# Expert stage: order of a tile's weights, the small slots' weights, the gates and the routing; gate weights moved behind attention

## The chip, the cores and the metric
The kernel runs on one core of a Trainium2 chip. Its time is the device time of one launch in microseconds; the kernel before has a median of 972.35 us over 3 runs (971.67 to 975.25). The engines are TensorE (PE, its weight loads as PEld), VectorE (DVE), ScalarE (ACT), GpSimd (POOL) and SyncE (SP), which issues most DMAs.

## The reference
All of it is float32. Three layers follow one another on 4 batches of 576 positions (2304 tokens, model width 512):
- attention, 8 heads of 64: `softmax(q k^T / 8, causal) v`, mixed with a memory term `phi(q) M / (phi(q) z + 1e-6)` by a gate per head, `g * mem + (1 - g) * local`, with g the sigmoid of `beta`;
- a dense layer: `h = x @ w_in` (512 to 2048), `h * clip(h + 3, 0, 6) / 6`, `@ w_out` (back to 512);
- an expert layer with 8 experts: `e = argmax(x @ w_gate)`, and for the tokens of expert e `gate_w * sigmoid(x @ w_output_gate[e]) * (relu(x @ w1[e]) @ w2[e])`, where `gate_w` is the softmax of the logits at e. Each w1 is 512x1024, each w2 1024x512.

## The kernel before, in words
**Accuracy.** A matmul operand is kept as two parts, high and low (names ending in H and L), and a product is three matmuls: high by high, high by low, low by high. For an expert's weights ACT casts the staged chunk to the high part (`high`, line 641) and DVE subtracts to get the low part (`low`, line 646).

**Attention and the first half of the dense layer** run together, from about 0 to 380 us. The order of their instructions on each engine is found by a planner from the program order, not written by hand. The gate weights `wg` (lines 409 to 411) are loaded near the start, cast on ACT and split on DVE into `wgs`; they are read for the first time by the logits in the second half of the dense layer, at 487 us.

**Routing.** After the last token block, `route()` counts the tokens of each expert, gives each token a slot, and makes index lists: `idx` (the rows that a tile of 128 tokens gathers), `idxs` (where its results go), `ei` and `sw` (a tile's expert, and whether it differs from that of the tile ahead of it). Nearly all of it is short DVE instructions. `route()` is a generator: each `next(routing)` runs it to the next `yield`, so the calls say between which matmuls its pieces stand. The two tiles of the expert that is found most loaded early (tiles 0 and 1) are computed beside it. `gates()` is the last token block's rest: a product with the gate's logits, an exponential on ACT (line 576), a reciprocal, and the store of the rows to `x2d`, from which the tiles gather.

**Tiles.** From `tiles(2, NR, ...)` on, tile i is computed while the weights of tile i + 1 are split. A tile is two groups of 12 matmuls for the hidden layer (`hidden`, line 688), two transposes of its result (line 667) and 24 matmuls for the output (`result`, line 701). `w.fetch` has SP issue 8 DMAs of 512 KB into staging buffers `st`; each has a condition, and where the next tile has the same expert it moves nothing. Its issue waits until the split has read the buffer for the last time. From here on the order on ACT, DVE, POOL and PE is the program's (`manual_schedule`); SP's is the planner's.

**Small slots.** An expert whose last tile holds at most 32 tokens gives these to one of four slots. Slot s is computed inside tile 4, 6, 9 or 11 (`HOSTS`). `small(s)` is a generator too: up to its first `yield` it reads the slot's expert (`esm`) on SP, gathers 32 rows (`sx`, POOL) and issues four loads of 512 KB (`sw<-w`, line 1020; the tile name `sw` is used twice). This is done one tile ahead. Each `tick()` in the host tile then runs one step: transposes, the hidden matmuls (line 1038) and the loads of the other four chunks (line 1022), a relu on ACT (`hq`, line 1043), transposes back, and the output matmuls (line 1056). A host tile has 17 ticks.

The lists of the slots (`idr`, `idq`, `esm`) are made in the last piece of `route()`, which runs at the end of tile 2.

Of the kernel before, what the change touches and what calls it, by code (L numbers as in the profile page):

```python
# [11 lines left out]
F32 = DT.float32  # L12
# [5 lines left out]
ALU = mybir.AluOpType  # L18
AX = mybir.AxisListType
# [3 lines left out]
P = 128  # L23
B, H, S, D = 4, 8, 576, 64
NT, DM, DFF = B * S, H * D, 2048
E, FF = 8, 1024
# [4 lines left out]
NS, SQ, SB = 4, 32, 4  # L31
NI = 24

NR = 19
HOSTS = {4: 0, 6: 1, 9: 2, 11: 3}
# [42 lines left out]
def f32(ap):  # L78
    return ap.bitcast(F32)
# [3 lines left out]
def tile_kernel(ctx, tc, qT, kT, qn, vx, z, beta, w_in, w_out, w_gates, w1, w2, out):  # L83
    nc = tc.nc
    PE, DVE, ACT, POOL, SP = nc.tensor, nc.vector, nc.scalar, nc.gpsimd, nc.sync
# [320 lines left out]
    DVE.memset(pz[:, :, D:], 1e-6)  # L406
    pairs[0].load()
    SP.dma_start(bt, beta.rearrange("(o h) -> o h", o=1).to_broadcast([P, H]))
    SP.dma_start(wg, w_gates.rearrange("(k p) e -> p k e", p=P))
    ACT.copy(wgs[:, :, : 2 * E], wg)  # L410
    DVE.tensor_tensor(wgs[:, :, 2 * E :], wg, f32(wgs[:, :, : 2 * E]), op=ALU.subtract)
    ACT.activation(gt, bt, AF.Exp, bias=0.0, scale=-1.0)
    DVE.tensor_scalar(gt, gt, 1.0, None, op0=ALU.add)
    DVE.reciprocal(gt, gt)
# [60 lines left out]
    for t in range(-1, len(pairs)):  # L475
        for x in PROGRAM.split():
            act(t, x)
    for _ in it:
        pass
    manual.close()  # L480
# [10 lines left out]
    k = 0  # L491
# [22 lines left out]
    part1, got = [], {}  # L514
# [98 lines left out]
    class Weights:  # L613
# [24 lines left out]
        def high(self, *cs):  # L638
            for c in cs:
                self.H[c] = self.pool.tile([P, 1024], F32R, name=f"wH{c}")  # L640
                ACT.copy(self.H[c], stage[c])  # L641
# [100 lines left out]
    def mid(x, n):  # L742

        return x.rearrange("p (o e) -> p o e", o=1).to_broadcast([P, n, x.shape[1]])

    def flat(x):
        return x.rearrange("p a b -> p (a b)")
# [72 lines left out]
    def route():  # L820
# [14 lines left out]
        DVE.tensor_reduce(cnt, tot, axis=AX.X, op=ALU.add)  # L835
        DVE.tensor_copy(tt, tot)
        DVE.tensor_tensor(gtc, cnt.to_broadcast([P, E, NJ]), mid(io18, E), op=ALU.is_gt)
        yield
        DVE.tensor_tensor_scan(flat(inc), onef, flat(tt), 0.0, op0=ALU.mult, op1=ALU.add)
        DVE.tensor_reduce(ntl, gtc, axis=AX.X, op=ALU.add)  # L840
# [33 lines left out]
        DVE.tensor_scalar(ci, pos, P - 1, None, op0=ALU.bitwise_and)  # L874
        DVE.tensor_scalar(ti, pos, 7, None, op0=ALU.arith_shift_right)
        DVE.tensor_copy(cf, ci)

        c1, c2 = (r2.tile([P, NI, E], F32, name=x) for x in ("c1", "c2"))
        DVE.tensor_tensor(c1, mid(flat(base), NI), itl.to_broadcast([P, NI, E]), op=ALU.is_le)
        DVE.tensor_copy(tf, ti)  # L880
        DVE.tensor_tensor(c2, mid(flat(end), NI), itl.to_broadcast([P, NI, E]), op=ALU.is_le)
        gates = got["gates"]
        next(gates)
        yield
        DVE.tensor_tensor(ohc[:, 0:6], mid(io128, 6), cf[:, 0:6].to_broadcast([P, 6, P]), op=ALU.is_equal)
        next(gates)
        DVE.tensor_tensor(c1, c1, c2, op=ALU.subtract)
        next(gates)
        DVE.tensor_tensor(ohc[:, 6:12], mid(io128, 6), cf[:, 6:12].to_broadcast([P, 6, P]), op=ALU.is_equal)
        next(gates)  # L890
        DVE.tensor_tensor(c1, c1, mid(io8, NI), op=ALU.mult)
        next(gates)
        yield
        DVE.tensor_tensor(ohc[:, 12:], mid(io128, NJ - 12), cf[:, 12:].to_broadcast([P, NJ - 12, P]), op=ALU.is_equal)
        yield
        ef = r2.tile([P, NI + 1, 1], F32, name="ef")
        DVE.memset(ef[:, 0:1], 0.0)
        DVE.tensor_reduce(ef[:, 1 : NI + 1], c1, axis=AX.X, op=ALU.add)
        rh = r2.tile([P, NJ, 3, NI + NS], BF16, name="rh")
        DVE.tensor_tensor(rh[:, :, 0], mid(ion, NJ), tf.to_broadcast([P, NJ, NI + NS]), op=ALU.is_equal)  # L900
        DVE.tensor_copy(ei, flat(ef)[:, 1 : NI + 1])
        DVE.tensor_tensor(sw, flat(ef)[:, 1 : NI + 1], flat(ef)[:, 0:NI], op=ALU.not_equal)
        DVE.tensor_scalar(rh[:, :, 1], rh[:, :, 0], iop, None, op0=ALU.mult)
        DVE.tensor_tensor(rh[:, :, 2], rh[:, :, 0], ioj.rearrange("p (j o) -> p j o", o=1).to_broadcast([P, NJ, NI + NS]), op=ALU.mult)
        yield
# [7 lines left out]
        DVE.scalar_tensor_tensor(tok, iv[:, 2], float(P), iv[:, 1], op0=ALU.mult, op1=ALU.add)  # L913
        DVE.tensor_copy(idx, tok)

        DVE.tensor_scalar(iv[:, 0], iv[:, 0], -1.0e6, 1.0e6, op0=ALU.mult, op1=ALU.add)
        DVE.tensor_tensor(tok, tok, iv[:, 0], op=ALU.add)
        DVE.tensor_copy(idxs, tok)
# [1 line left out]

        ivs = r.tile([P, 3, NS], BF16, name="ivs")
        DVE.tensor_copy(ivs, inv3[:, :, NI:])
        inq = ps_g.tile([P, 512], F32, name="inq", tag="pg")[:, : 3 * NS]
        PE.matmul(inq, lhsT=four, rhs=ivs.rearrange("p a n -> p (a n)"), start=True, stop=True)
        iq = r.tile([P, 3, NS], F32, name="iq")
# [5 lines left out]
        DVE.scalar_tensor_tensor(tks, tks, float(P // SQ), iq[:, 0], op0=ALU.mult, op1=ALU.add)  # L931
        DVE.tensor_scalar(tks, tks, qf, None, op0=ALU.add)
        DVE.tensor_copy(idq, tks)
        c3 = r.tile([P, NS, E], F32, name="c3")
        DVE.tensor_tensor(c3, mid(flat(key), NS), ion[:, 1 : NS + 1].rearrange("p (n o) -> p n o", o=1).to_broadcast([P, NS, E]), op=ALU.is_equal)
        DVE.tensor_tensor(c3, c3, mid(io8, NS), op=ALU.mult)
        ef3 = r.tile([P, NS, 1], F32, name="ef3")
        DVE.tensor_reduce(ef3, c3, axis=AX.X, op=ALU.add)
        DVE.tensor_copy(esm, flat(ef3))
        yield  # L940


# [46 lines left out]
    def hidden_out():  # L989
        return hp_.tile([P, FF], F32, name="hs"), [hp_.tile([P, 8, P], F32R, name=f"h{x}") for x in "HL"]  # L990
# [15 lines left out]
    def small(s):  # L1006


        er = SP.value_load(esm[0:1, s : s + 1], min_val=0, max_val=E - 1)
        xg = smp.tile([P, ROW], F32, name="sx")  # L1010
        POOL.indirect_dma_start(out=xg, out_offset=None, in_=x2d[:NT, :], in_offset=bass.IndirectOffsetOnAxis(ap=idr[:, s : s + 1], axis=0),
                                bounds_check=NT - 1, oob_is_err=False)
        ws = []

        def fetch():
            c = len(ws)
            if c < 2 * KD:
                w = smp.tile([P, 1024], F32, name="sw", bufs=SB)
                if c < KD:
                    SP.dma_start(w, w1[bass.ds(er, 1), c * P : (c + 1) * P, :].rearrange("o p f -> (o p) f"))  # L1020
                else:
                    SP.dma_start(w.rearrange("p (k d) -> p k d", k=2),
                                 w2[bass.ds(er, 1), 2 * (c - KD) * P : 2 * (c - KD + 1) * P, :].rearrange("o (k p) d -> (o p) k d", p=P))
                ws.append(w)

        for _ in range(SB):
            fetch()
        yield
        px = ps_g.tile([P, 512], F32, name="px", tag="pg")[:, : KD * SQ].rearrange("p (k t) -> p k t", k=KD)
        for k in range(KD):  # L1030
            PE.transpose(px[:, k], xg[:SQ, k * P : (k + 1) * P], ident[:SQ, :SQ])
        xT = smp.tile([P, KD, SQ], F32, name="xT")
        ACT.copy(xT, px)
        yield
        ph = ps_g.tile([P, 512], F32, name="ph", tag="pg")[:, : FF // 4]
        for k in range(KD):
            for g in range(4):
                PE.matmul(ph[g * SQ : (g + 1) * SQ, :], lhsT=xT[:, k], rhs=ws[k][:, g * 256 : (g + 1) * 256], start=k == 0, stop=k == KD - 1)
        while len(ws) < 2 * KD:
            fetch()  # L1040
        yield
        hq = smp.tile([P, FF // 4], F32, name="hq")
        ACT.activation(hq, ph, AF.Relu)
        yield
        pt = ps_g.tile([P, 512], F32, name="pt", tag="pg")[:, : 2 * P]
        for c in range(2):
            PE.transpose(pt[:, c * P : (c + 1) * P], hq[:, c * P : (c + 1) * P], ident)
        hT = smp.tile([P, 2, P], F32, name="hT")
        ACT.copy(hT, pt.rearrange("p (c t) -> p c t", c=2))
        for _ in range(9):  # L1050
            yield
        py = ps_g.tile([P, 512], F32, name="py", tag="pg")[:, :P]
        for g in range(4):
            for c in range(2):
                for q in range(4):
                    PE.matmul(py[q * SQ : (q + 1) * SQ, :], lhsT=hT[:, c, g * SQ : (g + 1) * SQ], rhs=ws[KD + g][:, c * 512 + q * P : c * 512 + (q + 1) * P],
                              start=g + c == 0, stop=g + c == 4)
        yield
        ys = smp.tile([P, P], F32, name="sy")
        ACT.activation(ys, py, AF.Copy, scale=xg[:, DM : DM + 1])  # L1060
        POOL.indirect_dma_start(out=out.rearrange("n (q d) -> (n q) d", q=4), out_offset=bass.IndirectOffsetOnAxis(ap=idq[:, s : s + 1], axis=0),
                                in_=ys, in_offset=None, bounds_check=4 * NT - 1, oob_is_err=False)
        yield
# [7 lines left out]
    def stepped(g, n):  # L1071

        for _ in range(n):
            r_ = next(g)
            tick()
        return r_

    def tiles(i0, i1, w, xg, xn, xx):
        nonlocal beside, smp
        for i in range(i0, i1):  # L1080
            if i + 1 in HOSTS and i + 1 < i1:
                ahead = small(HOSTS[i + 1])
                next(ahead)
            if i in HOSTS:
                beside = ahead
            more = i + 1 < i1
# [3 lines left out]
            xnn = rows(idx[:, i + 2 : i + 3]) if i + 2 < i1 else None  # L1090
            if more:
                w.fetch(0, 1, 2, 3, 4, 5, 7, 6)
            high, low = (w.high, w.low) if more else (lambda *cs: None,) * 2

            hs, hh = hidden_out()
            tick()
            ph = stepped(hidden(w0, xx, 0), 4)
# [8 lines left out]
            low(2)  # L1106
            DVE.tensor_tensor(hh[1][:, 0:4], px, f32(hh[0][:, 0:4]), op=ALU.subtract)
            ph = stepped(g, 2)
            high(3)
            relu(hs, ph, 1)  # L1110
            low(3)
# [108 lines left out]
```

## Time and profile before
| | |
|---|---|
| profiled execution | 975.48 us |
| its span, first to last instruction | 973.4 us |
| median of 3 runs | 972.35 us |
| PE busy | 915.6 us, 94% of the span |
| DVE, ACT, POOL busy | 627.7, 519.3, 370.5 us |
| mean granted TensorE clock | 0.978 |

The profile counts an instruction as busy from its start to its end; for PE, whose matmuls are pipelined, ends are modelled. "Idle before" is the time in which the engine had nothing running ahead of an instruction, and the name behind the arrow is what ended it. The granted clock of a stretch is a share of 2.4 GHz.

### The profile page before, as it was taken

How to read it: one execution, taken by the hardware profiler on the slowest of the kernel's cores; microseconds unless marked ns; L12 is line 12 of the kernel's file. 1: busy time of each engine (PE TensorE's matmuls, PEld its weight loads, DVE VectorE, ACT ScalarE, POOL GpSimd, SP SyncE). 2: the span in 40 equal slices, each digit the busy share in tenths (PEclk: the TensorE clock that was granted, in tenths of full speed). 3: DMA queues.
4: the chain of work that ended last, by engine and by line, in shares of the span. 5: the costliest groups of instructions: out<-in, count | busy, mean ns of one | idle time of the engine just before them, and what ended most of it. 6: DMA issues, size and time to landing. Idle time of an engine off the chain costs nothing. (4 is left out here: it accounts for less than half of the span.)

```text
span 973.4 us, 17053 instructions
## 1 busy us (share of the span) xinstructions
PE 915.6 (94%) x5733; PEld 721.7 (74%) x5733; DVE 627.7 (64%) x1511; ACT 519.3 (53%) x1084; POOL 370.5 (38%) x574
## 2 busy tenths in 40 slices
PE   5788889999999999899999999998997999999996
PEld 3445667777777778779988888887775777778785
DVE  6889996576556533686344444448766769668982
ACT  5677665565555454444222222223345768668883
POOL 2636556465555443245433333336021212112210
PEclk9989899999999999899999999999999999999998
DMA  5434432121212003443011111113223664633850
GB/s 181 139 112 146 131 100 74 52 86 52 78 54 90 14 23 109 130 131 108 1 45 44 44 44 45 44 44 138 80 77 120 218 250 176 208 131 119 311 205 23
DMA packets 49277, 101.69 MB, mean 104 GB/s; under 512 B 5341, under 2 KB 15581, under 8 KB 49184
## 3 DMA queue, kind: packets, MB, share of 16 engines
q1 hardware_dynamic: 45696, 89.74, 27.3%
q0 software_dynamic: 3488, 10.80, 3.3%
q8 instruction: 47, 0.77, 0.3%
q14 instruction: 46, 0.38, 0.1%
HBM read 136.66 MB, written 14.72 MB: 156 GB/s over the span
## 5 line engine op out<-in xcount | busy, mean ns | idle before, releaser
L646 DVE TENSOR_TENSOR wL<-st,wH 128x1024 fp32r<-128x1024 f32 x136 | 163.7, 1227 | 42.7 <-ACT wH L641 41.5
L95 POOL TENSOR_SCALAR gH<-g 128x256 fp32r<-128x256 f32 x144 | 65.5, 455 | 271.4 <-DVE g L217 213.5
L213 PE MATMUL hps<-xH,wH 128*128 128x256 f32 x576 | 167.3, 291 | 1.5 <-ACT xH L91 1.0
L213 PE MATMUL hps<-xL,wH 128*128 128x256 f32 x576 | 163.0, 283 | 2.4 <-DVE xL L200 2.4
L213 PE MATMUL hps<-xH,wL 128*128 128x256 f32 x576 | 161.7, 281 | 0.0
L365 POOL TENSOR_SCALAR a<-a,rs,omg 128x320 f32<-128x320 f32 (+4 forms) x160 | 128.1, 812 | 78.0 <-DVE rs L360 52.1
L217 DVE SCALAR_TENSOR_TENSOR g<-g,hps 128x256 f32<-128x256 f32 x144 | 60.0, 417 | 146.4 <-ACT g L216 146.4
L641 ACT CAST wH<-st 128x1024 fp32r<-128x1024 f32 x136 | 139.7, 1053 | 8.4 <-DMA st<-w 8.3
L216 ACT ACTIVATE g<-hps,half 128x256 f32<-128x256 f32 x144 | 68.1, 473 | 139.2 <-PE hps L213 116.0
L213 PEld LDWEIGHTS hps<-xH,wH 128*128 128x128 f32 x576 | 109.5, 191 | 18.3 <-issue 12.6
L221 POOL TENSOR_TENSOR gL<-g,gH 128x256 fp32r<-128x256 f32 x144 | 115.8, 804 | 11.7
L213 PEld LDWEIGHTS hps<-xL,wH 128*128 128x128 f32 x576 | 109.8, 191 | 8.4 <-DVE xL L200 3.4
L352 ACT ACTIVATE a<-st,mn 64x64 f32<-64x64 f32 (+4 forms) x160 | 88.4, 555 | 43.9 <-DVE mn L343 43.8
L213 PEld LDWEIGHTS hps<-xH,wL 128*128 128x128 f32 x576 | 109.8, 191 | 0.1
L182 PE MATMUL acc<-wH,gH 128*128 128x512 f32 x288 | 95.8, 414 | 0.2 <-POOL gH L95 0.2
L337 PE MATMUL pa<-kd,qd 64*128 64x64 f32 (+5 forms) x384 | 82.1, 470 | 13.8 <-DVE mn L343 8.7
L182 PE MATMUL acc<-wH,gL 128*128 128x512 f32 x288 | 91.6, 400 | 2.3 <-POOL gL L221 2.3
L182 PE MATMUL acc<-wL,gH 128*128 128x512 f32 x288 | 91.0, 398 | 0.0
L376 PE MATMUL pa<-ident,a 128*128 128x128 f32 (+1 forms) x480 | 75.3, 289 | 13.3 <-DVE mn L343 8.0
L376 PEld LDWEIGHTS pa<-ident,a 128*128 128x128 f32 (+1 forms) x480 | 55.6, 145 | 37.1 <-DVE mn L343 14.0
L708 POOL DMA_INDIRECT out<-ys,idxs x17 | 19.2, 1128 | 124.7 <-ACT ys L707 69.4
L182 PEld LDWEIGHTS acc<-wH,gL 128*128 128x128 f32 x288 | 54.3, 190 | 15.9 <-POOL gL L221 3.1
(239 smaller groups left out, 1720.8 us busy)
## 6 DMA issues: line engine op xcount, KB each, us to landing
st<-w SPq DMA_DIRECT2D x136, 512.0 KB
sw<-w SPq DMA_DIRECT2D x32, 512.0 KB
w<-w_in SPq DMA_DIRECT2D x16, 512.0 KB
w<-w_out SPq DMA_DIRECT2D x16, 512.0 KB
qnt<-qn SPq DMA_DIRECT2D x16, 320.0 KB
vt<-vx SPq DMA_DIRECT2D x16, 320.0 KB
x2d<-row SPq DMA_DIRECT2D x18, 258.0 KB
qd<-qT SPq DMA_DIRECT2D x16, 288.0 KB
```

The costliest lines, as they stand in the source:

```text
L95: POOL.tensor_scalar(out, x, 1.0, 1.0, op0=ALU.mult, op1=ALU.mult)
L182: PE.matmul(acc[t], lhsT=gg[:, t * P : (t + 1) * P], rhs=ww[:, 512:1024], start=m == 0 and first, stop=m == HM - 1 and last)
L213: PE.matmul(hps, lhsT=ww[:, kk * P : (kk + 1) * P], rhs=xx[:, kk], start=k == 0, stop=k == 3 * KD - 1)
L216: ACT.activation(g, hps, AF.Relu, bias=half, scale=1.0 / 6.0)
L217: DVE.scalar_tensor_tensor(g, g, 1.0, hps, op0=ALU.min, op1=ALU.mult)
L221: ENG[GL].tensor_tensor(gL, g, f32(gH), op=ALU.subtract)
L337: PE.matmul(pss[j][: QN[i], o : o + k1 - k0], lhsT=self.qd[r, QS[i] : QS[i] + QN[i]], rhs=self.kd[r, k0:k1], start=True, stop=True)
L352: ACT.activation(self.a[j][:m, o + D : o + D + n], self.st[j][i][:m, :n], AF.Exp, bias=self.mn[j][:m, i : i + 1], scale=-1.0, accum_out=se ...
L365: ENG[NORM[i]].tensor_scalar(av, av, r[:m, i], omg[:m, h : h + 1], op0=ALU.mult, op1=ALU.mult)
L376: PE.transpose(psa[:, off : off + QN[i]], self.a[j][: QN[i], QO[i] + c * P : QO[i] + (c + 1) * P], ident[: QN[i], : QN[i]])
L641: ACT.copy(self.H[c], stage[c])
L646: DVE.tensor_tensor(self.L[c], stage[c], f32(self.H[c]), op=ALU.subtract)
```

## The change
- `wg` is loaded, cast and split behind the program of attention instead of near the start.
- In `route()`, `gates()` begins in the second piece instead of the third, and the instructions that make `ei` and `sw` (lines 879 to 902) stand behind those that make `idx`.
- The slots' lists get two pieces instead of one: `esm` first, `idr` and `idq` second. They are run in tile 2 ahead of its first and of its second half's `high(3)`.
- One tile ahead of a host, `w.fetch` comes first, then the put and the gather of the tile, and `small(...)` behind them.
- In the host, the slot's relu and transposes come four ticks later, and its output matmuls one tick later.

```diff
     SP.dma_start(bt, beta.rearrange("(o h) -> o h", o=1).to_broadcast([P, H]))
-    SP.dma_start(wg, w_gates.rearrange("(k p) e -> p k e", p=P))
-    ACT.copy(wgs[:, :, : 2 * E], wg)
-    DVE.tensor_tensor(wgs[:, :, 2 * E :], wg, f32(wgs[:, :, : 2 * E]), op=ALU.subtract)
...
             act(t, x)
+    SP.dma_start(wg, w_gates.rearrange("(k p) e -> p k e", p=P))
+    ACT.copy(wgs[:, :, : 2 * E], wg)
+    DVE.tensor_tensor(wgs[:, :, 2 * E :], wg, f32(wgs[:, :, : 2 * E]), op=ALU.subtract)
...
         DVE.tensor_tensor(gtc, cnt.to_broadcast([P, E, NJ]), mid(io18, E), op=ALU.is_gt)
+        gates = got["gates"]
+        next(gates)
         yield
...
-        c1, c2 = (r2.tile([P, NI, E], F32, name=x) for x in ("c1", "c2"))
-        DVE.tensor_tensor(c1, mid(flat(base), NI), itl.to_broadcast([P, NI, E]), op=ALU.is_le)
         DVE.tensor_copy(tf, ti)
-        DVE.tensor_tensor(c2, mid(flat(end), NI), itl.to_broadcast([P, NI, E]), op=ALU.is_le)
-        gates = got["gates"]
-        next(gates)
         yield
...
         DVE.tensor_copy(idx, tok)
+        c1, c2 = (r2.tile([P, NI, E], F32, name=x) for x in ("c1", "c2"))
+        DVE.tensor_tensor(c1, mid(flat(base), NI), itl.to_broadcast([P, NI, E]), op=ALU.is_le)
+        DVE.tensor_tensor(c2, mid(flat(end), NI), itl.to_broadcast([P, NI, E]), op=ALU.is_le)
+        DVE.tensor_tensor(c1, c1, c2, op=ALU.subtract)
+        DVE.tensor_tensor(c1, c1, mid(io8, NI), op=ALU.mult)
+        ef = r2.tile([P, NI + 1, 1], F32, name="ef")
+        DVE.memset(ef[:, 0:1], 0.0)
+        DVE.tensor_reduce(ef[:, 1 : NI + 1], c1, axis=AX.X, op=ALU.add)
+        DVE.tensor_copy(ei, flat(ef)[:, 1 : NI + 1])
+        DVE.tensor_tensor(sw, flat(ef)[:, 1 : NI + 1], flat(ef)[:, 0:NI], op=ALU.not_equal)
...
         DVE.tensor_copy(ivs, inv3[:, :, NI:])
+        c3 = r.tile([P, NS, E], F32, name="c3")
...
+        DVE.tensor_copy(esm, flat(ef3))
+        yield
         inq = ps_g.tile([P, 512], F32, name="inq", tag="pg")[:, : 3 * NS]
...
         while len(ws) < 2 * KD:
             fetch()
         yield
+        for _ in range(4):
+            yield
         hq = smp.tile([P, FF // 4], F32, name="hq")
...
-        for _ in range(9):
+        for _ in range(6):
             yield
...
         for i in range(i0, i1):
-            if i + 1 in HOSTS and i + 1 < i1:
-                ahead = small(HOSTS[i + 1])
-                next(ahead)
             if i in HOSTS:
                 beside = ahead
...
             if more:
                 w.fetch(0, 1, 2, 3, 4, 5, 7, 6)
+            if i + 1 in HOSTS and i + 1 < i1:
+                ahead = small(HOSTS[i + 1])
+                next(ahead)
             high, low = (w.high, w.low) if more else (lambda *cs: None,) * 2
+            if i == 2:
+                next(routing)
             hs, hh = hidden_out()
...
             ph = stepped(g, 2)
+            if i == 2:
+                next(routing)
             high(3)
```

## Rows read from the trace of the kernel before
**Rows 1.** Busy time by stretch: PE, PEld, DVE, ACT, POOL, clock, DMA share, GB/s.
```profile
884.92:898.29 13.37, 13.37 (x67) 10.82 (x66) 11.93 (x13) 11.59 (x15) 2.52 (x2) 1.00 0.32 117
```
**Rows 2.** PE's waits from 655 us on: total us, times, longest.
```profile
PE px L667 <- ACT hs L693: 7.7, 6, 3.8
...
PE py L701 <- DVE hL L1107: 1.1, 4, 0.3
```
**Rows 3.** Timeline in tile 3: start, length, engine, line, operation [idle before, releaser].
```profile
736.64 2.08 SPq L1020 DMA_DIRECT2D sw<-w  x4
...
739.14 13.97 SPq L636 DMA_DIRECT2D st<-w  x16
739.23 1.99 ACT L641 CAST wH<-st 128x1024 fp32r<-128x1024 f32 x2 [6.32 <-DMA st<-w]
...
741.77 0.66 PE L667 MATMUL px<-ident,hs 128*128 128x128 f32 x4 [3.84 <-ACT hs L693]
```
**Rows 4.** Timeline of the routing, beside tile 1.
```profile
703.79 0.35 DVE L879 TENSOR_TENSOR c<-base,itl 128x192 f32<-128x192 f32 x1
...
704.81 0.20 ACT L576 ACTIVATE so<-so 128x2 f32<-128x2 f32 x1 [8.00 <-DVE so L575]
...
706.13 0.66 PE L667 MATMUL px<-ident,hs 128*128 128x128 f32 x4 [0.85 <-ACT hs L693]
...
710.81 0.85 PE L908 MATMUL inv<-rh,ohc 128*128 128x84 bf16 x18 [1.40 <-DVE rh L904]
```
**Rows 5.** Timeline in tile 4, the first host.
```profile
756.81 0.37 ACT L1049 COPY hT<-pt 128x256 f32<-128x256 f32 x1 [1.40 <-PE pt L1047]
...
759.63 0.66 PE L667 MATMUL px<-ident,hs 128*128 128x128 f32 x4 [0.76 <-ACT hs L693]
```
**Rows 6.** Timeline at the end of tile 2, where the slots' lists are made.
```profile
733.25 0.17 DVE L922 CAST ivs<-inv 128x12 bf16<-128x12 f32 x1
733.47 0.17 PE L924 MATMUL inq<-ivs,four 128*128 128x12 bf16 x1 [1.29 <-DVE ivs L922]
...
735.56 0.17 DVE L939 CAST esm<-ef 128x4 int32<-128x4 f32 x1
```
**Rows 7.** Busy time by single microseconds behind that stall, the clock among it.
```profile
742.00:743.00 1.00, 1.00 (x7) 0.91 (x6) 0.97 (x2) 1.00 (x2) 0.00 (x0) 0.88 0.93 360
743.00:744.00 1.00, 1.00 (x4) 0.71 (x4) 1.00 (x2) 1.00 (x2) 0.00 (x0) 0.50 1.03 422
...
746.00:747.00 1.00, 1.00 (x8) 0.76 (x7) 0.80 (x1) 0.17 (x1) 0.00 (x0) 0.92 0.29 99
```
**Rows 8.** Timeline of POOL around the second host's gather.
```profile
769.10 1.02 POOL L1061 DMA_INDIRECT out<-sy,idq  x1 [13.86 <-ACT sy L1060]
...
775.30 2.00 POOL L708 DMA_INDIRECT out<-ys,idxs  x1 [3.37 <-ACT wH L641]
```
**Rows 9.** Timeline at the start of the kernel.
```profile
2.67 0.43 SPq L408 DMA_DIRECT2D bt<-beta  x1
3.15 0.43 SPq L409 DMA_DIRECT2D wg<-w_gates  x1
...
9.23 0.24 ACT L410 CAST wgs<-wg 128x64 fp32r<-128x64 f32 x1 [2.68 <-DMA wg<-w_gates]
...
9.65 0.17 DVE L413 TENSOR_SCALAR gt<-gt 128x8 f32<-128x8 f32 x1
```
**Rows 10.** Busy time behind the start, columns as in rows 1.
```profile
20.00:140.00 120.00, 99.37 (x571) 64.15 (x570) 109.22 (x325) 79.53 (x209) 64.77 (x96) 0.91 0.40 127
```
**Rows 11.** The slots' gathers: from issue to landing.
```profile
DMA to landing us min/median/max: 4.7/6.2/7.4
```
**Rows 12.** Busy time by stretch, from the loads ahead of three hosts on.
```profile
764.00:782.00 18.00, 18.00 (x143) 14.48 (x142) 14.48 (x15) 14.35 (x19) 5.99 (x4) 1.00 0.45 164
...
803.00:826.00 23.00, 23.00 (x112) 18.50 (x111) 20.82 (x21) 20.34 (x26) 6.23 (x5) 1.00 0.50 187
842.00:858.00 16.00, 16.00 (x109) 12.96 (x98) 12.80 (x14) 13.24 (x18) 4.57 (x4) 1.00 0.54 184
```

More of the change, by code (lines that the diff above doesn't have):

```diff
@@ L886, in route @@
         next(gates)
-        DVE.tensor_tensor(c1, c1, c2, op=ALU.subtract)
         next(gates)
@@ L890, in route @@
         next(gates)
-        DVE.tensor_tensor(c1, c1, mid(io8, NI), op=ALU.mult)
         next(gates)
@@ L895, in route @@
         yield
-        ef = r2.tile([P, NI + 1, 1], F32, name="ef")
-        DVE.memset(ef[:, 0:1], 0.0)
-        DVE.tensor_reduce(ef[:, 1 : NI + 1], c1, axis=AX.X, op=ALU.add)
         rh = r2.tile([P, NJ, 3, NI + NS], BF16, name="rh")
         DVE.tensor_tensor(rh[:, :, 0], mid(ion, NJ), tf.to_broadcast([P, NJ, NI + NS]), op=ALU.is_equal)
-        DVE.tensor_copy(ei, flat(ef)[:, 1 : NI + 1])
-        DVE.tensor_tensor(sw, flat(ef)[:, 1 : NI + 1], flat(ef)[:, 0:NI], op=ALU.not_equal)
         DVE.tensor_scalar(rh[:, :, 1], rh[:, :, 0], iop, None, op0=ALU.mult)
@@ L922, in route @@
         DVE.tensor_copy(ivs, inv3[:, :, NI:])
+        c3 = r.tile([P, NS, E], F32, name="c3")
+        DVE.tensor_tensor(c3, mid(flat(key), NS), ion[:, 1 : NS + 1].rearrange("p (n o) -> p n o", o=1).to_broadcast([P, NS, E]), op=ALU.is_equal)
+        DVE.tensor_tensor(c3, c3, mid(io8, NS), op=ALU.mult)
+        ef3 = r.tile([P, NS, 1], F32, name="ef3")
+        DVE.tensor_reduce(ef3, c3, axis=AX.X, op=ALU.add)
+        DVE.tensor_copy(esm, flat(ef3))
+        yield
         inq = ps_g.tile([P, 512], F32, name="inq", tag="pg")[:, : 3 * NS]
@@ L933, in route @@
         DVE.tensor_copy(idq, tks)
[L934 to L939, printed above, removed]
         yield
```

## The prediction
> **What bounds the kernel now.** I read the busy shares first: PE works for 94% of the span, so a change pays only where PE stands still or its clock is low. Next came busy time by stretch. A stretch of plain tiles has PE busy without a gap at full clock, DVE for 11.93 of 13.37 us and ACT for 11.59 [rows 1]: nothing that shortens DVE, ACT or DMA there moves the end. Then PE's waits from the routing on: it waits six times, 7.7 us in all, for `hs` from ACT, longest 3.8, and four times, 1.1 us, for the low part of `hs` from DVE [rows 2]. The timeline says where. One wait is tile 3's, 3.84 [rows 3]; one is the routing's, 0.85 [rows 4]; the other four, 0.76 each, are the hosts' [rows 5] (3.84 + 0.85 + 4 x 0.76 = 7.73). The reader is to see that each is a question of order on a queue: in none of them is the engine that PE waits for short of time.
>
> **The change part by part.** The sum is made against the profiled execution, 975.48 us (span 973.4); the median is 3.13 lower.
>
> *Tile 3.* SP issues the first slot's loads at 736.64, then tile 4's weights at 739.14. ACT had stood idle for 6.32 us and begins at 739.23, 0.09 after that first issue: these DMAs move nothing (same expert), so ACT waited for their issue and for no bytes. Its cast stands ahead of `relu` on ACT, and so PE waits 3.84 until 741.77 [rows 3]. SP stood behind `esm`, which DVE wrote at 735.56 [rows 6], because `small` came first in the program. With the fetch first, these eight issues wait only for their staging buffers, which the split frees during tile 2. The 3.84 goes. So does what follows it: the granted clock is 0.88 in the microsecond from 742, 0.50 in the three from 743 (the first stands) and 0.92 in that from 746 [rows 7], 2.4 GHz falling to 1.2 after the idle stretch. What is missing to 1 there is lost: 0.12 + 3 x 0.50 + 0.08 = 1.7. Sum 5.5. Nothing else is late there: tile 3's rows were gathered in the routing, and the slot's inputs are wanted only a tile later.
>
> *End of tile 2.* `inq` on PE waits 1.29 us for `ivs`, queued on DVE behind the last low parts [rows 6]. Both lists now come earlier in tile 2, and that wait goes. The price: seven short DVE instructions of 0.17 (as the cast of `esm` [rows 6]), 1.2 us, now stand in front of `low(3)` in a tile where DVE has little idle time. The low part of the second half of `hs` comes about 1.2 later, and its matmul is the seventh behind the transposes: I estimate some 0.7 to spare and take 0.5 lost, bounds 0 and 1.2. Net 0.8 (0.1 to 1.3).
>
> *Routing.* `so` on ACT waits 8.00 us for DVE, with `ys` and `hs` behind it, and PE waits 0.85 [rows 4]. With `gates` begun one piece earlier that wait goes. It is not an extra gain: PE then reaches the matmuls of `inv` sooner and waits there, as it does now, 1.40 for `rh` [rows 4]. What moves `inv` is DVE's chain. Eight instructions leave it; five of them go over 192 columns, 0.35 each [rows 4], at most 1.75 end to end; ends overlap the next one's start, and the three small ones are left out. The three DVE instructions of `gates` stay in the chain, so moving them is worth nothing by itself. I take 1.3. Behind `idx` the moved instructions delay the low part of `hs` that `result` wants; PE loses there what a full clock could have won, so 0.9 to 1.9. `ei` and `sw` come some 3 us later on SP, and tile 3's fetch with them; it moves nothing, and its first cast stands behind `ys`, so it is covered.
>
> *Hosts.* ACT waits 1.40 for the slot's transposes [rows 5], with `high(0, 1)` and `relu` queued behind; PE then waits 0.76 for `hs` and 0.3 for the low part [rows 2, 5]. Four ticks later, `hq` stands behind `relu` and `high(2)`, where its matmuls are long done. Four hosts: 4 x 1.04 = 4.2. ACT has two more short copies (0.37 each, as `hT` [rows 5]) in front of `high(3)` and the second `relu`, which I price at 0.15 a host: 3.6 (2.5 to 4.2). The output matmuls one tick later still have three ticks.
>
> *Slots' inputs.* The loads now stand behind the tile's eight issues, the last of which waits for the last low part, so they go out some 5 to 7 us later than at 736.64 and its like; 2.1 MB at 422 GB/s [rows 7] take 5 us, and they are wanted a whole tile after. On POOL the gather stands behind the put and the tile's gather. At the second host the put waits for the slot's stores: from 769.10 to 775.30 [rows 8]. I cost both at nothing, cover about 1 us for the gather and 3 for the loads; without it PE, strictly in order here, stands still.
>
> *Start.* ACT waits 2.68 for `wg`, then casts it for 0.24 ahead of `gt`, and DVE's `gt` begins at 9.65 [rows 9]. Of the 120 us from 20 on DVE is busy for 109.22, PE for 99.37 [rows 10]: DVE is the nearest to full there, and I let the start's gain pass on whole. Next in line is `bt`. If that lands only as `wg` does, 0.2 is won; if it is there when ACT would first ask, at 6.55 (9.23 less 2.68), it is 2.85 (9.65 less 6.8). `bt` was issued 0.48 ahead of `wg` [rows 9], and I give it that lead: 0.7. The split behind attention is 0.5 us of work on two engines that have slack there, long ahead of its reader. The planner's order may shift elsewhere; I have no row for that and let the range bear 1.5 either way.
>
> Sum: 5.5 + 0.8 + 1.3 + 3.6 + 0.7 = 11.9. The profiled execution becomes 963.6, the median 972.35 - 11.9 = 960.5.
>
> **The rivals.**
> 1. *The fetch still comes late.* SP's order is the planner's; it could still issue `sw` ahead of `st`. For it: SP is not among the engines ordered by hand. Against it: before, SP followed the program, `sw` then `st` [rows 3]. Without 5.5 the median is 966.0.
> 2. *The slots' gather is late.* Last on POOL, behind a put that waited 6.2 us for the slot's stores [rows 8], it would be issued some 8 us into the tile and land 7.4 later at worst [rows 11], 15.4. It is wanted when the tile ends: 60 matmuls at 13.37 / 67 each [rows 1] are 12.0, with the joints some 12.4. PE stands 3 at hosts two and four, with 1.7 each of half clock as in tile 3: 9.4, so 970; at the median landing of 6.2 it is 3.6, so 964. Against it: that put waited while the slot's loads filled the DMA engines, and these now come later. The Trainium skill (DMA: Bandwidth & Descriptors, section Queues, rings and completion order) says that each DMA engine takes turns between the queues by packet; by that a gather would not wait for all of the loads in front of it, and this rival would cost little. The landings of 4.7 to 7.4 agree in that none is as long as the loads.
> 3. *More at the start*: `bt` there at once, 2.85, and 1.9 in the routing: 2.8 more, 957.7.
> 4. *The order of loads turns against the hosts: slower.* Where the tile after really changes expert, 4.2 MB now go ahead of the slot's 2.1 MB: 10 us at 422 GB/s in front of loads with 3 us to spare. PE would stand some 7 us a host. Two hosts eat the gain, from there on it is slower; four cost 28 and give 988. For it: the loads are now behind. Against it: ahead of the second to fourth host 18 us at 164 GB/s are 3.0 MB, 23 at 187 are 4.3 and 16 at 184 are 2.9 [rows 12]; the loads and the rows of the tiles fill these, the middle one with the end of an earlier tile's fetch, so no fetch of 4.2 MB stands there, nor at the first host [rows 3].
> 5. *No change*: rivals 1 and 2 together, 11.9 - 5.5 - 5 to 6 = about 1, so 971.
>
> **How the numbers follow.** Forecast 0.61, rival 1 0.09, rival 2 0.11, rival 3 0.10, rival 4 0.04, rival 5 0.05. A measurement of this kernel tells 0.5% (4.9 us) from no change. Faster: the forecast and rivals 1 to 3, less 0.01 for the worst of rival 2, 0.90. Same: 0.06. Slower: 0.04. The forecast's own range is 956.5 to 963.5. At the low end stands 956 (between the forecast and all its bounds at once, 957.7 less the hosts' 0.6 and the planner's share); the high end takes in rival 1 and the milder rival 2, 967.5.
>
> **What would show it.** In the changed trace: tile 4's `st` issued by SP ahead of the first `sw`, no wait of ACT for `st`, PE's waits for `hs` down from 7.7 to under 1, full clock through tiles 2 to 4; `inq` inside tile 2; the `inv` matmuls about 2 us earlier against the kernel's start (1.3 of the routing's and 0.7 of the start's); each host about 0.9 shorter. A wait of PE for `sx` or the slot's `sw` would show rivals 2 or 4; the first block of dense matmuls coming later than before would say that the planner's new order costs more than the start gives.

## The result, and the profile after

The changed kernel takes 962.05 us (median of 4 runs, 960.27 to 963.5), the kernel before beside it 972.01: ratio 0.9889, 95% interval 0.9862 to 0.9917. Timed again it took 962.99 us (6 runs, 959.75 to 965.45) against 974.09, ratio 0.9887 [0.986, 0.9913]. So 10 to 11 us were won. The profiled execution is 961.85 us, its span 959.9.

PE's waits from 640 us on, of the kernel after (engine and line, what it waited for: total us, times, longest):

```profile
PE acc L182 <- POOL gL L221: 2.3, 1, 2.3
PE py L701 <- DVE hL L672: 1.5, 2, 0.8
PE inv L897 <- DVE rh L893: 1.1, 1, 1.1
PE pi L815 <- DVE ohc L812: 0.6, 1, 0.6
PE py L701 <- ACT hH L671: 0.4, 1, 0.4
PE pf L760 <- DVE ohb L822: 0.4, 1, 0.4
```

Against [rows 2], both of those waits are gone: no `px` for `hs`, 7.7 before, and no `py` for the low part of the hosts' `hs`. Two new ones stand in the list, both in the routing: 1.5 for a low part (L672) and 0.4 for a high part (L671).

SP's queue in tiles 2 to 4, and, with the columns of [rows 1], the stretch in which the granted clock (third from the end) had been 0.50 to 0.92 [rows 7]:

```profile
714.66 17.66 SPq L636 DMA_DIRECT2D st<-w  x16
733.18 2.14 SPq L1021 DMA_DIRECT2D sw<-w  x4
736.91 7.81 SPq L636 DMA_DIRECT2D st<-w  x8
```
```profile
742.00:746.00 4.00, 4.00 (x42) 2.49 (x44) 3.30 (x4) 3.68 (x6) 1.23 (x2) 1.00 0.02 7
```

The sixteen `st` of tiles 3 and 4 are issued before the first `sw`; before, tile 4's stood behind it [rows 3]. The profile's group of ACT's casts shows what that ended: idle before them 2.0 us in all, 1.9 of it for `st`; before, it was 8.4 and 8.3. Tile 3's 6.3 of it is gone. What is left stands ahead of 712 us, and so do the 3.6 of a second profile of the changed kernel.

```profile
L641 ACT CAST wH<-st 128x1024 fp32r<-128x1024 f32 x136 | 139.6, 1052 | 2.0 <-DMA st<-w 1.9
```

The slots' lists in tile 2, and the first host (answers to [rows 6] and [rows 5]):

```profile
719.07 0.31 DVE L928 CAST esm<-ef 128x4 int32<-128x4 f32 x1
...
723.73 0.18 PE L931 MATMUL inq<-ivs,four 128*128 128x12 bf16 x1
```
```profile
748.96 0.60 ACT L693 ACTIVATE hs<-ph 128x512 f32<-128x512 f32 x1 [2.71 <-PE ph L688]
...
750.10 0.60 PE L667 MATMUL px<-ident,hs 128*128 128x128 f32 x4
750.39 0.39 ACT L1046 ACTIVATE hq<-ph 128x256 f32<-128x256 f32 x1
...
751.66 0.37 ACT L1052 COPY hT<-pt 128x256 f32<-128x256 f32 x1 [0.33 <-PE pt L1050]
...
752.88 0.61 ACT L693 ACTIVATE hs<-ph 128x512 f32<-128x512 f32 x1
...
753.55 0.64 PE L667 MATMUL px<-ident,hs 128*128 128x128 f32 x4
```

`inq` has no bracket: PE stands idle for nothing in front of it. ACT waits 0.33 for the slot's transposes, not 1.40. The transposes at 750.10 are those that waited 0.76 for `hs` before [rows 5]; the first `hs` now stands ahead of the slot's relu on ACT, and PE doesn't wait. Nor does it at 753.55, the transposes of the second half, whose `hs` now has the slot's copies in front of it.

Where the time went, stage by stage. Marks: DVE's first row sum of the dense layer's second half (483.06 us in the profile before), its last one (685.36), and the end of a tile, which is the start of ACT's `ys`; the last row ends with that of the last tile. Gains in us, against the profile of before; the second column is a second profile of the changed kernel.

| stage | predicted | profile after | second profile |
|---|---|---|---|
| to the first row sum (start) | 0.7 | -0.35 | -0.12 |
| to the last row sum | 0 | 1.42 | -0.10 |
| to the end of tile 1 (routing) | 1.3 | 0.63 | 0.08 |
| tile 2 | -0.5 | -0.38 | -0.39 |
| tile 3 | 5.5 + 1.3 | 7.06 | 7.03 |
| to the end of the last tile (four hosts) | 3.6 | 5.28 | 5.27 |
| sum | 11.9 | 13.66 | 11.77 |

The two profiles differ where the clock does. Busy time and clock of the two places, before, after, and after once more:

```profile
681.00:685.00 4.00, 3.50 (x11) 2.86 (x12) 0.69 (x1) 1.39 (x2) 1.56 (x3) 0.57 1.05 402
712.00:716.00 4.00, 4.00 (x14) 3.19 (x13) 1.46 (x6) 0.59 (x1) 2.05 (x2) 0.57 0.35 82
```
```profile
681.00:685.00 4.00, 3.15 (x16) 2.57 (x16) 1.54 (x4) 1.94 (x3) 1.91 (x3) 1.00 1.04 400
712.00:716.00 4.00, 3.17 (x14) 2.26 (x13) 2.10 (x10) 0.25 (x1) 1.55 (x2) 1.00 0.47 132
```
```profile
681.00:685.00 4.00, 3.17 (x10) 2.64 (x11) 0.64 (x2) 1.06 (x2) 1.88 (x3) 0.57 1.04 402
712.00:716.00 4.00, 4.00 (x14) 3.21 (x13) 3.35 (x15) 0.58 (x1) 2.15 (x2) 0.57 0.27 70
```

The first profile after had full clock in both stretches; the second had, like the kernel before, half clock for most of each (0.57 over 4 us is 4 x 0.43 / 0.5 = 3.4 us at 0.50). So like stands against like in the last column, and the 1.42 and 0.63 of the first are not the change's.

### The profile page after: what moved, and what is told of

The parts are those of the page before. It is cut to its first block, busy times and chain, and to the rows that moved or that the text cites. A ratio compares the mean times of both kernels' runs of the same rounds, so it can differ in the third digit from the quotient of the medians.

```text
span 959.9 us, 17064 instructions
## 1 busy us (share of the span) xinstructions
PE 909.2 (95%) x5733; PEld 717.6 (75%) x5733; DVE 630.3 (66%) x1511; ACT 519.2 (54%) x1084; POOL 370.5 (39%) x574
```

## The experiments

**The kernel before, profiled again** (no edit).

> The kernel before, unchanged, profiled a second time. Theory A (the gain of the two profiled executions, 13.6 us, is larger than that of the medians, 10.0, because the first profile of before happened to have its clock at 1.2 GHz from 681.3 and from 712.0 us, which most executions do not): span about 970 us, granted clock 1.00 from 680 to 686 and from 711 to 716, the dip from 742.8 still there. Theory B (those two dips belong to the work in front of them): both dips again, span 973 to 974.

976.8 us. The half clock came back in both places:

```profile
681.00:685.00 4.00, 2.66 (x8) 2.24 (x9) 0.70 (x1) 0.55 (x2) 2.39 (x3) 0.65 0.98 375
712.00:716.00 4.00, 4.00 (x26) 3.33 (x23) 1.73 (x7) 0.59 (x1) 2.04 (x2) 0.62 0.20 45
```

Theory B held for this kernel. But the second profile of the changed kernel has the same two, so the change did not remove them: whether they come differs between executions of one kernel.

**The changed kernel, profiled and timed again** (no edit).

> The changed kernel once more, beside the others of this job. Theory A (its two half-rate stretches less in the routing are a matter of chance between executions): span 959 to 963, one or both dips near 681 and 712 back. Theory B (its order of work keeps the clock up there): no dip near 712, tile 1's stretch 33.1 again; ratio to before 0.988 to 0.989.

962.99 us, as above; the half clock stood at both places this time.

**Later ticks alone, on the kernel before.**

```diff
         yield
+        for _ in range(4):
+            yield
         hq = smp.tile([P, FF // 4], F32, name="hq")
...
-        for _ in range(9):
+        for _ in range(6):
             yield
```

> The kernel before with only the slot's relu and transposes four ticks later and its output matmuls one tick later. Theory A (ACT, held by the slot's transposes, is the only thing that delays the hosts): each host tile 1.3 us shorter (18.9 to 17.6), 5.3 in all, tile 3 still 19.7 long; time about 0.9945 of before. Theory B (hosts also need the loads in the new order, or later ticks meet late loads): less than 3 us.

969.13 us, ratio 0.9945 [0.9929, 0.9961]. Each host is 1.34 us shorter, 5.4 in all, and tile 3 stays at 19.6. Theory A: PE's `px` waits fall from six times to two,

```profile
PE px L667 <- ACT hs L693: 4.5, 2, 3.7
```

which are tile 3's and the routing's.

**The order of the loads alone, on the kernel before.**

```diff
-            if i + 1 in HOSTS and i + 1 < i1:
-                ahead = small(HOSTS[i + 1])
-                next(ahead)
...
                 w.fetch(0, 1, 2, 3, 4, 5, 7, 6)
+            if i + 1 in HOSTS and i + 1 < i1:
+                ahead = small(HOSTS[i + 1])
+                next(ahead)
```

> The kernel before with only the tile's fetch put ahead of the small slot one tile before a host. Theory A (tile 3 stands for the issue of the fetch alone): tile 3 shorter by 3.84 of idle, 0.17 of pipelining and 1.7 of half clock, 5.7 in all (19.7 to 14.0, the wait for the slots' lists of 1.3 stays); hosts unchanged at 18.9; time 0.994 of before. Theory B (the slot's loads or gather, now later while the lists are still made at the end of tile 2, arrive late): tile 3 shorter, but a wait for the slot's rows or loads in tile 4 gives 1 us or more back.

968.5 us, ratio 0.9932 [0.9912, 0.9951]. Tile 3 takes 14.17 us, not 19.66: 5.49, hosts unchanged at 18.88. Of the waits for `hs`, tile 3's alone has gone:

```profile
PE px L667 <- ACT hs L693: 3.9, 5, 0.8
...
PE inq L924 <- DVE ivs L922: 1.3, 1, 1.3
```

The 1.3 of `inq` is still there; in the full change tile 3 wins 7.03, the 1.5 more that the earlier list gives. This profile had full clock at 712 and takes 32.27 us from the last row sum to the end of tile 1: that, not the 33.74 of before, is what the new routing has to be held against where the clock is full.

**`wg` back at the front, in the changed kernel.**

```diff
     SP.dma_start(bt, beta.rearrange("(o h) -> o h", o=1).to_broadcast([P, H]))
+    SP.dma_start(wg, w_gates.rearrange("(k p) e -> p k e", p=P))
+    ACT.copy(wgs[:, :, : 2 * E], wg)
+    DVE.tensor_tensor(wgs[:, :, 2 * E :], wg, f32(wgs[:, :, : 2 * E]), op=ALU.subtract)
...
-    SP.dma_start(wg, w_gates.rearrange("(k p) e -> p k e", p=P))
-    ACT.copy(wgs[:, :, : 2 * E], wg)
-    DVE.tensor_tensor(wgs[:, :, 2 * E :], wg, f32(wgs[:, :, : 2 * E]), op=ALU.subtract)
```

> The changed kernel with the gate weights loaded and split near the start again. Theory A (beta lands as late without the gate weights, so moving them wins nothing): gt on DVE at 9.6 to 9.7, second half of the dense layer within 0.5 us of the changed kernel's, time the same within 0.1%. Theory B (the load behind attention wins the 0.7 that was forecast): 0.7 us slower than the changed kernel.

963.66 us, ratio 0.9877 [0.986, 0.9894], against 0.9887 and 0.9889 with the move: the time shows no worth of moving `wg`, though 0.7 us, 0.0007, is less than the interval could show. Theory A's marks were missed: `gt` begins on DVE at 10.21, not at 9.6 to 9.7, and the first row sum comes at 484.67, 1.3 to 1.5 behind the changed kernel's two profiles. Single profiles scatter as widely: the first row sum comes at 482.42 to 484.67 in the five with `wg` in front (mean 483.33) and at 482.26 to 483.41 in the four with it moved and `bt` where it was (mean 482.96).

**`bt` loaded first, in the changed kernel.**

```diff
-    pairs[0].load()
     SP.dma_start(bt, beta.rearrange("(o h) -> o h", o=1).to_broadcast([P, H]))
+    pairs[0].load()
```

> The changed kernel with beta's load issued ahead of all others. Theory A (beta's landing, not the gate weights, holds the start, and a gain there passes on): gt on DVE at about 7.7 instead of 9.65, and the first row sum of the dense layer's second half 1.5 to 2 us earlier, at 481.5 to 482. Theory B (the attention stage gives it back, as its chain runs through ACT, PE and POOL too): gt as early, but that row sum within the 482.4 to 483.9 that profiles of the unchanged order show.

> The changed kernel with the load of bt issued ahead of the first rows' loads, timed. In its profile ACT had bt by 3.85 us instead of 9.41, and the second dense half's first row sum came at 479.81 us, against 483.41 and 483.18 in the two profiles of the changed kernel. Theory A (bt behind the first rows' loads holds DVE's first work, and what that costs passes on whole to the end): some 3 us below the changed kernel, a ratio to the kernel before of about 0.985. Theory B (the time at 483 us scatters from run to run by 2 us in any case, and a single profile shows nothing): a ratio of 0.988 to 0.989, as the changed kernel.

959.09 us in the one run; timed 960.79 (958.98 to 961.66), ratio 0.9862 [0.9836, 0.9888]. `gt` comes on DVE at 4.09, far ahead of the 7.7 expected. The start, of the changed kernel and of this one:

```profile
2.67 0.43 SPq L408 DMA_DIRECT2D bt<-beta  x1
...
9.41 0.21 ACT L409 ACTIVATE gt<-bt 128x8 f32<-128x8 f32 x1 [2.39 <-DMA bt<-beta]
9.53 0.72 ACT L289 ACTIVATE phi<-phi 128x640 f32<-128x640 f32 x1
...
10.28 0.82 DVE L292 SCALAR_TENSOR_TENSOR phi<-qnt,phi 128x640 f32<-128x640 f32 x1
```
```profile
0.80 0.40 SPq L407 DMA_DIRECT2D bt<-beta  x1
...
3.85 0.21 ACT L409 ACTIVATE gt<-bt 128x8 f32<-128x8 f32 x1 [1.76 <-DMA bt<-beta]
...
8.02 0.83 DVE L292 SCALAR_TENSOR_TENSOR phi<-qnt,phi 128x640 f32<-128x640 f32 x1 [3.32 <-ACT phi L289]
```

`gt` stands on ACT ahead of `phi`, so a late `bt` holds DVE's first long instruction: 10.28 against 8.02. The first row sum comes at 482.26 to 484.67 us in the nine profiles with `bt` behind the first loads (mean 483.17) and at 479.62 to 482.08 in the four with it first (mean 480.63). The sets don't overlap, though only 0.18 lies between them, and the means are 2.5 us apart: the row sum comes earlier, as Theory A has it. That this passes on whole to the end is not shown. The time is 1.3 to 2.2 us below the changed kernel's 962.05 and 962.99, not 3, and the interval of the ratio overlaps the changed kernel's.

**`gates` begun behind the split, in the changed kernel.**

```diff
+        yield
         gates = got["gates"]
         next(gates)
-        yield
```

> The changed kernel with the start of gates one piece later still, behind the split of the second half of hs: on ACT the exponential then stands behind that cast instead of in front of it. Theory A (in the changed kernel that cast waited for the exponential and for DVE, and held DVE's chain by 0.7): the scan comes 0.7 to 0.8 earlier against the last row sum, and the stretch from that sum to the end of tile 1 is 32.4 us instead of 33.1. Theory B (the chain is bound by DVE's own work, its place on ACT is worth nothing): 33.0 or more.

959.7 us in one run. First the changed kernel's routing, then this one's:

```profile
696.82 0.21 ACT L576 ACTIVATE so<-so 128x2 f32<-128x2 f32 x1 [2.81 <-DVE so L575]
696.93 0.57 ACT L671 CAST hH<-px 128x512 fp32r<-128x512 f32 x1
697.53 0.69 DVE L672 TENSOR_TENSOR hL<-px,hH 128x512 fp32r<-128x512 f32 x1 [0.74 <-ACT hH L671]
...
697.55 0.50 PE L701 MATMUL py<-wH,hH 128*128 128x512 f32 x1 [0.39 <-ACT hH L671]
...
698.14 0.45 DVE L841 TENSOR_TENSOR_SCAN inc<-onef,tt 128x144 f32<-128x144 f32 x1
```
```profile
693.90 0.59 ACT L671 CAST hH<-px 128x512 fp32r<-128x512 f32 x1 [1.07 <-PE px L667]
696.24 0.20 ACT L576 ACTIVATE so<-so 128x2 f32<-128x2 f32 x1 [1.75 <-DVE so L575]
```

In the changed kernel `so` stands ahead of `hH` on ACT and waits 2.81 for DVE; `hH`, its low part on DVE, PE and then the scan of the routing stand behind. With `gates` behind the split, `hH` goes first. From the last row sum, the scan starts after 13.00 us (changed kernel 13.85 and 13.91, before 12.79) and the `inv` matmuls after 24.36 (25.27 and 25.34, before 25.45); the end of tile 1 comes after 32.20, not 33.11, both at full clock: Theory A.

**The tiles' expert list behind the low part, in the changed kernel.**

```diff
         DVE.tensor_copy(idx, tok)
+        yield
...
     split4(px, hh, 4)
+    next(routing)
```

> The changed kernel with one edit: the tiles' expert list (c1 to sw) and idxs behind the low part of hs in tile 1, gates and bt as in the changed kernel. Theory A (those DVE instructions stand in front of the low part that PE's result matmuls want): PE's wait for the low part at L701 beside tile 1's second half goes, and from the last row sum to the end of tile 1 it takes 32.2 us instead of 33.1 with an undisturbed clock (33.7 with the half clock near 712). Theory B (PE would wait for the next tile's rows instead): 33.1 as before, and the wait is for xg.

961.85 us in one run. The end of tile 1 comes 32.06 us after the last row sum, without half clock at 712: Theory A. First the changed kernel, then this one:

```profile
713.50 0.34 DVE L918 CAST idxs<-tok 128x24 uint32<-128x24 f32 x1
713.59 0.68 DVE L672 TENSOR_TENSOR hL<-px,hH 128x512 fp32r<-128x512 f32 x1
...
714.33 0.50 PE L701 MATMUL py<-wH,hL 128*128 128x512 f32 x1 [0.83 <-DVE hL L672]
```
```profile
713.33 0.69 DVE L672 TENSOR_TENSOR hL<-px,hH 128x512 fp32r<-128x512 f32 x1 [1.16 <-ACT hH L671]
...
713.94 0.35 DVE L907 TENSOR_TENSOR c<-base,itl 128x192 f32<-128x192 f32 x1
```

Before, DVE's low part waited for ACT, as it does here; in the changed kernel it queues behind the moved instructions, and PE waits 0.83 for it. The edit takes the three instructions of `idxs` along, which stood ahead of the low part before the change too.

**The last three together, in the changed kernel.** The edits are those above. Timed twice.

> The changed kernel with the gates behind the cast, the experts' list behind the low part of hs (a further piece of the routing), and beta's load first. Theory A (these three are what the change left over): the stretch from the last row sum to the end of tile 1 about 31.4 (33.1 in the changed kernel), the start 0 to 2 earlier: 2 to 3.5 us below the changed kernel, 0.986 of before. Theory B (the rows' gather or a dip of the clock takes the place of these waits): within 1 us of the changed kernel.

> The changed kernel with gates back behind the split, bt first and the tiles' expert list behind the low part, timed over more rounds. Theory A (the three edits are worth 0.9, 3 and 0.9 us in the profiles, less 0.7 for the fourth slot's gather, which PE waited for there): about 1 us below the kernel with bt first alone, a ratio of 0.984. Theory B (what the routing gives is taken back by the slot's gather): the same ratio as with bt first alone, within 0.001.

958.62 us (955.96 to 961.02), ratio 0.9847 [0.9821, 0.9873], beside the changed kernel's 962.99; the second time 958.95 (957.42 to 961.86), ratio 0.9857 [0.9828, 0.9885], beside 960.79 with `bt` first alone. Five of the first six runs lie below the lowest of the changed kernel beside them; the intervals of the ratios overlap. From the last row sum to the end of tile 1 its two profiles take 31.29 and 31.22 us, against 33.17 with `bt` first alone at full clock there. In the first profile it paid something back at the fourth host,

```profile
843.08 0.43 PE L1033 MATMUL px<-ident,sx 32*128 32x32 f32 x4 [0.68 <-DMA sx<-x2d,idr]
```

rival 2's wait; the gather had been issued at 835.26, 5.4 us into the tile (4.1 in the changed kernel). The second profile has no such wait, though its gather was issued as late, 5.4 us into the tile, so the cover there is about nothing. Whether the routing's 1.9 us pass on whole to the time is left open: the ratios of the second time, with these edits and with `bt` first alone, differ by 0.0005, the medians by 1.84 us.

## Why the prediction was right, and where its terms were not

960.5 us was predicted, 962.05 and 962.99 measured, 1.6 to 2.5 above it; the forecast's mechanism is what happened. Its sum, 11.9, stands beside 11.77 in the profile of like clock, but two of its terms came out near nothing and one was half as large again. That the sum comes so near is luck in part: routing and start gave 2.0 less than forecast, the hosts 1.7 more. Later ticks alone (ratio 0.9945) and the order of loads alone (0.9932) already make up 0.9877 together; in the time the rest of the change added nothing that shows.

- *Tile 3, 5.5.* Right, and shown by itself: 5.49 with the order of loads alone. The stall went, and the half clock behind it: that stands in all three profiles with the stall, and the granted clock is 1.00 from 730 to 750 in the ten without it.
- *End of tile 2, 1.3 less 0.5.* Tile 2 lost 0.39 to the lists, and tile 3 won some 1.5 from `inq`: net 1.1 for 0.8. Most of the loss is the late low part that was foreseen: the first matmul of the second half that reads it starts 0.55 behind the one ahead of it, not 0.23 (at 728.28, profile after), with no idle shown.
- *Hosts, 3.6.* Too small: 1.33 each. The wait was worth more than its "idle before". In the kernel before, the matmuls ahead of the host's transposes start every 0.23 us, though each is drawn 0.40 long:

```profile
758.24 0.39 PE L688 MATMUL ph<-wL,xgH 128*128 128x512 f32 x1
...
758.47 0.40 PE L688 MATMUL ph<-wH,xgL 128*128 128x512 f32 x1
```

  The next started at 759.63 [rows 5]: 1.16 instead of 0.23, so 0.93 lost where the row says 0.76, as 0.17 of the wait lies under the drawn end of the matmul before. With the low part's wait, 0.45 by the same count, that is 1.38 a host. The 0.15 that I charged for ACT's copies was not paid: no wait for ACT is left there.
- *Routing, 1.3.* Failed: 0.08 with like clock, and 0.84 lost at full clock (33.11 against 32.27). Two steps were wrong. "The three DVE instructions of `gates` stay in the chain, so moving them is worth nothing by itself" looked at DVE alone; on ACT the move puts `so` ahead of `hH`, and that costs 0.9. And the price of the list ahead of the low part, put at 0.4 at most, is 1.05 with that of `idxs` (33.11 to 32.06). The gain from the shortened chain exists: with `gates` behind the split, `inv` comes 1.09 earlier than before.
- *Start, 0.7.* Failed. `bt` was given a lead of 0.48 over `wg` because it was issued that much ahead of it. `gt` begins on DVE at 9.65 to 10.21 in the five profiles with `wg` in front (mean 9.93) and at 9.46 to 9.91 in the four without (mean 9.71): 0.2, the low case of the term, in which `bt` lands only as `wg` does. The row sums' means say 0.4, single ones scatter by 2.4, so the -0.35 and -0.12 of the table decide nothing. (The planner has SP issue the moved `wg` at 12.86 us and ACT cast it at 21.2: ahead of most of attention.) It is behind the first rows' loads that `bt` lands late, and putting it ahead of them is worth 2.5 at the first row sum, near the 2.85 that the prediction gave for a `bt` that is there at once.
- *Slots' inputs, nothing.* Right for the changed kernel: in neither of its profiles does PE wait for `sx` or `sw`. The loads did not go out 5 to 7 us later throughout: from the start of the tile ahead of the host, SP issues them 2.1 us earlier than before for the first slot, 7.0 later for the second and fourth, and 12.2 later for the third. The kernel with three more edits shows how thin the cover of the gather is.

The rivals: SP's order rules out 1 and 5. Rival 2 needs a wait for `sx`, rival 4 one for `sw`; there is none, and all four hosts became shorter by the same 1.33. One reason is on POOL: the put ahead of the second host started 6.2 us after the slot's store [rows 8], and now 3.0. Of the 6.2 some 2.3 passed before its own `ys` was done (770.76, with 0.69 of work).

```profile
759.44 1.02 POOL L1064 DMA_INDIRECT out<-sy,idq  x1 [11.99 <-ACT sy L1063]
762.47 1.01 POOL L708 DMA_INDIRECT out<-ys,idxs  x1 [2.02 <-ACT ys L707]
```

The order of loads does it: alone, on the kernel before, it gives 3.0 (761.83 to 764.87), later ticks alone 6.9 (767.01 to 773.90). It moves the slot's loads and its gather behind the put together; which of the two counts is not shown. Rival 3 came true in neither part.

## What to carry to other kernels

When a piece of an in-order program is moved, read the queue of every engine it issues to, at the new place: an activation of 0.2 us on ACT and a list of short instructions on DVE each cost about 1 us by standing ahead of something PE wanted. Count a PE wait from start to start of its matmuls. And before crediting a load with an earlier landing, ask which loads it is queued behind.

## What the hardware showed that was not expected

- A load of 4 KB (`bt`) issued at 2.67 us behind four larger loads let its reader start at 9.41; issued first, at 0.80, at 3.85. The Trainium skill (DMA: Bandwidth & Descriptors, section "Two DMAs through the same engine are not ordered") says that within one queue of a DMA engine descriptors start in order; these two runs agree with it, though none tells that rule from a plain shortage of bandwidth.
- Half clock at about 681 and 712 us comes in some executions of a kernel and not in others, behind the same wait: PE stands 2.3 to 2.5 us for `gL` just ahead of the one place and 1.1 to 1.4 for `rh` ahead of the other, in the profiles with the fall (ten of thirteen at 681, five at 712) and in those without. At 681 the fall goes with 1.4 us (202.2 to 202.4 us between the two row sums with it, 200.9 without). At 712 it goes with 1.5 in the old order of the routing (33.74 against 32.27) and 0.5 in the new (33.66 against 33.11). In the new order PE waits 1.5 for low parts at full clock and 0.7 at half, so part of what the slow clock costs had been lost already.
